# Binding one stage's weight conversion to its place in each engine's order, and three smaller edits, in a fused attention and feed-forward kernel

## The chip, the cores and the metric

One core of one Trainium2 chip. The metric is device time in microseconds (us) of one launch of the kernel, the median of several runs. TensorE (PE, with PEld for its weight loads) does the matrix products, VectorE (DVE) and ScalarE (ACT) the elementwise work, and SyncE (SP) issues every data transfer of this kernel, in order, from one queue.

## The reference, cut to what matters

```python
# attention: 4 batches, 8 heads, 512 local and 32 global tokens, head size 64
out_g = softmax(q_g @ k_all.T / 8) @ v_all                  # global queries see every key
out_l = softmax([q_l @ k_g.T, masked(q_l @ k_l.T)] / 8) @ v # local ones: |i - j| <= 32, and the global keys
x = rows(out_g, out_l)                                      # 2304 tokens x 512

h = x @ w_in                                                # layer 1: 512 -> 2048 -> 512
x = (np.maximum(h, 0.0) + alpha * np.minimum(h, 0.0)) @ w_out

h = x @ w_in2                                               # layer 2, with its own weights
return (h * np.clip(h + 3.0, 0.0, 6.0) / 6.0) @ w_out2
```

The weights arrive as 64-bit floats, the rest as 32-bit.

## The kernel before, in words

A matrix operand is held in two parts, a high one (rounded to TensorE's 32-bit form) and a low one (the remainder), and one product is three matrix products of the parts. Weights are first made 32-bit floats from the two words of each 64-bit number (`to_float32`, L100: ACT L108, then DVE L111, L112, L114), then split (ACT cast, DVE subtract).

Layer 1 goes over the tokens in five blocks (main loop, L776 to L828) of 512, 512, 512, 256 and 384 columns. A block's step s computes `h` (PE, L365) for one of 16 chunks of the hidden width; `act` (L370) takes it through ACT L375, DVE L377, ACT L383 and DVE L384 into a split tile `g`; two steps later (`LAG`) `y` (PE, L396) adds that chunk's share to four banks. Between the steps `attention_steps` issues pieces of the attention of later blocks: scores (L184), softmax (DVE L192, ACT L196), transposes (L207, copied by ACT L209 into `pt`), values (L219, scaled by DVE L223). At a block's end the attention results are transposed (L350) and split (L336, L337) into `xt` for the next block, and the four `y` banks are copied out (`evacuate`, L402: ACT L407 and DVE L405 in turn, through the ring of tiles `t`, TB = 3) and stored in DRAM, one store for each bank (L827). Block 0 also converts layer 1's own weights, which stay on the chip. Block 3 carries the global attention, and block 4 the splits (`inputs`, L552) that layer 2 starts from.

Layer 2's weights are converted during layer 1 by a generator, `second_weights` (L449): 32 chunks, each loaded (L97), converted, split and stored back to DRAM (L468) for layer 2 to read. The first 16 chunks go in pairs and make two more tiles per pair (`parts`; L471 adds, L459 cast, L462 subtract). The main loop draws some of its 158 pieces at each step; `SPLIT` = (0, 46, 46, 30, 37) says how many in each block. Layer 2 (L659) is TensorE work over these stored parts, and `rest` (L741 to L759) treats the last block's 384 tokens and ends the kernel (L634, `to_rows` L637).

Three rings of buffers matter: `raw`, four tiles that the loaded weights, the `parts` tiles and later some of layer 2's weights share; `z`, two; and `g`, three.

The order in which each engine executes is not the order of the code. The context is made with a timeline simulation (L883), and the scheduler puts each engine's instructions in the order in which that simulation finds them ready, so a piece of the generator may stand well ahead of the block step behind which it was drawn.

Of the kernel before, what the change touches and what calls it, by code (L numbers as in the profile page):

```python
# [9 lines left out]
F32 = mybir.dt.float32  # L10
F32R = mybir.dt.float32r
U32 = mybir.dt.uint32
I64 = mybir.dt.int64
AF = mybir.ActivationFunctionType
ALU = mybir.AluOpType
# [7 lines left out]
NC = DM // 128  # L23
# [4 lines left out]
UNIT_K = 15 * W  # L28

LAG = 2  # L30
# [3 lines left out]
PRE = 3  # L34
# [1 line left out]
SKEW = 1  # L36
ZB = 2
WARM = 8
TB = 3
DELAY = 4  # L40
STEPS = [[2] * 4 + [1] * 16, [1] * 16, [1] * 16, [2] * 16, [0] * 16]
CONVERT = (5, 7, 9)
# [10 lines left out]
def fused_kernel(ctx, tc, qT, kE, vE, qgT, kN, vN, vgN, w1, alpha, w2, mask, ident, out):  # L53
    nc = tc.nc
# [4 lines left out]
    work = pool("work")  # L59
# [37 lines left out]
        nc.sync.dma_start(out=raw, in_=src[j, :, 512 * m:512 * m + 512])  # L97
        return raw

    def to_float32(raw):  # L100

        words = raw.bitcast(U32).rearrange("p (f two) -> p f two", two=2)
        low, high = words[:, :, 0], words[:, :, 1]
        nc.scalar.activation(low, low, AF.Relu, bias=quarter_sb, scale=0.9 * 2.0 ** -29)  # L108
        z = work.tile([128, 512], F32, tag="z", name="z", bufs=ZB)
        bits = z.bitcast(U32)  # L110
        nc.vector.tensor_scalar(out=z, in0=high.bitcast(F32), scalar1=2.0 ** -112, scalar2=None, op0=ALU.mult)  # L111
        nc.vector.scalar_tensor_tensor(out=bits, in0=bits, scalar=3, in1=low, op0=ALU.logical_shift_left,  # L112
                                       op1=ALU.bitwise_or)
        nc.vector.scalar_tensor_tensor(out=bits, in0=high, scalar=0x80000000, in1=bits, op0=ALU.bitwise_and,  # L114
                                       op1=ALU.bitwise_or)
        return z
# [41 lines left out]
    def local_units(att):  # L158
        units = [(b, hf, hp) for b in range(B) for hf in range(2) for hp in range(HP)]
        q_t, k_t, v_t, p_t, rs_t, pt_t = {}, {}, {}, {}, {}, {}  # L160
        def load(u):
            b, hf, hp = units[u]
            q_t[u] = att.tile([128, 256], F32, tag="q", name="q_t", bufs=PRE + 1)
            nc.sync.dma_start(out=q_t[u], in_=qT[b, hp, :, 256 * hf:256 * hf + 256])
            k_t[u] = att.tile([128, UNIT_K], F32, tag="kE", name="k_t", bufs=PRE)
            nc.sync.dma_start(out=k_t[u], in_=kE[b, hp, :, 384 * hf:384 * hf + UNIT_K])

        def load_v(u):
# [61 lines left out]
        n = len(units)  # L230
# [217 lines left out]

    def second_weights():  # L449

        todo = [(j, 0) for j in range(NJ)] + [(j, 1) for j in range(NJ)]
        raws, pending = [], []

        def fetch():
            if todo:
                raws.append(load_raw(w2, *todo.pop(0)))

        def high(z, st):
            nc.scalar.copy(st[:, 0:512], z)  # L459

        def low(z, st, dst):
            nc.vector.tensor_tensor(out=st[:, 512:1024], in0=z, in1=st[:, 0:512].bitcast(F32), op=ALU.subtract)  # L462
            pending.append((dst, st))

        def store():
            if pending:
                d, st = pending.pop(0)
                nc.sync.dma_start(out=d, in_=st.bitcast(F32))  # L468

        def add(out, a, b, op=ALU.add):  # L470
            nc.vector.tensor_tensor(out=out, in0=a, in1=b, op=op)  # L471

        def parts_tile():
            return work.tile([128, 512], I64, tag="raw", name="parts", bufs=RAW).bitcast(F32R)

        fetch()
        yield
        fetch()  # L480
        for _ in range(5):
            yield
        for m in range(NP):
            own = raws.pop(0)
            z0, own = to_float32(own), own.bitcast(F32R)
            yield
            high(z0, own)
            yield
            low(z0, own, in_parts[m][:, 0])
            yield  # L490
            own = raws.pop(0)
            z1, own = to_float32(own), own.bitcast(F32R)
            store()
            yield
            high(z1, own)
            yield
            low(z1, own, in_parts[m][:, 1])
            yield
            a, b, c, d = z0[:, 0:256], z0[:, 256:512], z1[:, 0:256], z1[:, 256:512]
            add(d, c, d)  # L500
            add(c, a, c, ALU.subtract)
            store()
            yield
            st = parts_tile()
            high(z1, st)
            yield
            low(z1, st, in_parts[m][:, 2])
            fetch()
            yield
            add(a, d, a, ALU.subtract)  # L510
            add(b, b, a, ALU.subtract)
            store()
            yield
            st = parts_tile()
            high(z0, st)
            yield
            low(z0, st, in_parts[m][:, 3])
            fetch()
            yield
            store()  # L520
            yield
        for j in range(NJ):
            own = raws.pop(0)
            z, own = to_float32(own), own.bitcast(F32R)
            store()
            yield
            high(z, own)
            fetch()
            yield
            low(z, own, out_parts[j])  # L530
            yield
        store()
# [87 lines left out]
    def take(*key):  # L620
        ahead(STREAM + RAW - 2)
        return stream["got"].pop(key)
# [5 lines left out]
        nc.scalar.copy(g[:, 0, :], t)  # L628
        nc.vector.tensor_tensor(out=g[:, 1, :], in0=t, in1=g[:, 0, :].bitcast(F32), op=ALU.subtract)

    def outputs(y, g, wo, j):
        for c in range(len(y)):
            for wl, gl in ((0, 0), (1, 0), (0, 1)):
                nc.tensor.matmul(y[c], lhsT=g[:, gl, 128 * c:128 * c + 128], rhs=wo[:, wl, :],  # L634
                                 start=j == 0 and (wl, gl) == (0, 0), stop=j == NJ - 1 and (wl, gl) == (0, 1))

    def to_rows(y, tiles):  # L637
        for c, tile_ in enumerate(tiles):
            r = evacuate(y[c], c, 512, ("t", "z"))
            if tile_ == "g":  # L640
                nc.sync.dma_start(out=rows[:, 0:SG, :], in_=r)
            else:
                bb, hf, i = tile_
                at = SG + 256 * hf + 128 * i
                nc.sync.dma_start(out=rows[bb, at:at + 128, :], in_=r)
# [13 lines left out]
    def second_layer(bt):  # L659
# [14 lines left out]
        for n, two in enumerate(twos):  # L674
# [4 lines left out]
            gs, far = {}, []  # L679
# [65 lines left out]
        for j in range(NJ + LAG):  # L745
            if j < NJ:
                wt = take("in", n, j // 2, j % 2)
                h = fresh("h_ps")[:, 0:w]
                k = 0
                for c in range(NC):  # L750
                    for wl, xl in ((0, 0), (1, 0), (0, 1)):
                        nc.tensor.matmul(h, lhsT=wt[:, wl, 128 * c:128 * c + 128], rhs=xt[c][:, xl, 0:w], start=k == 0,  # L752
                                         stop=k == 3 * NC - 1)
                        k += 1
                gs[j] = g_tile()[:, :, 0:w]
                act2(h, gs[j], w)
            if j >= LAG:
                outputs(y, gs.pop(j - LAG), take("out", n, 0, j - LAG), j - LAG)
        to_rows(y, [(3, 1, 0), (3, 1, 1), "g"])  # L759

    W1 = Weights(w1, early=True)
    second, bt = second_weights(), {}
# [13 lines left out]
    for bi in range(len(blocks)):  # L776
# [43 lines left out]
        if last:  # L820
# [2 lines left out]
            for _ in more:  # L823
                pass
            ahead(STREAM + RAW - 2)
        for c in range(NC):
            nc.sync.dma_start(out=x2[bi][:, c, :], in_=evacuate(y[c], c, n)[:, :n])  # L827
        xt = xt_next  # L828

    second_layer(bt)  # L830
# [56 lines left out]
```

## Time and profile before

| | us |
|---|---|
| median of 3 runs | 899.4 (898.88 to 900.55) |
| the profiled execution | 899.25 |
| its span in the trace | 897.5 |
| PE busy in the span | 853.2 (95%) |
| DVE, ACT busy | 527.6 (59%), 392.2 (44%) |
| PE busy, 0 to 60 us (start of attention) | 49.15 |
| 60 to 165 (block 0) | 98.78 of 105 |
| 165 to 294 and 294 to 403 (blocks 1 and 2) | 114.45 of 129, 105.38 of 109 |
| 403 to 467.9 and 467.9 to 535 (blocks 3 and 4) | 64.23 of 64.9, 67.10 of 67.1 |
| 535 to 822 (layer 2), 822 to 889.2 (`rest`) | 286.86 of 287, 67.20 of 67.2 |
| mean granted TensorE clock | 0.974 |

The span is the traced part of one execution. A row of the timeline gives an instruction's start and length; the bracket at its end is the idle time of its engine just before it and what ended that. PEclk is the TensorE clock that was granted, as a share of full speed. "DMA raw<-in_w" is a load of a weight chunk, "DMA x<-ev" a store of a block's result.

### The profile page before, as it was taken

How to read it: one execution, taken by the hardware profiler on the slowest of the kernel's cores; microseconds unless marked ns; L12 is line 12 of the kernel's file. 1: busy time of each engine (PE TensorE's matmuls, PEld its weight loads, DVE VectorE, ACT ScalarE, POOL GpSimd, SP SyncE). 2: the span in 40 equal slices, each digit the busy share in tenths (PEclk: the TensorE clock that was granted, in tenths of full speed). 3: DMA queues.
4: the chain of work that ended last, by engine and by line, in shares of the span. 5: the costliest groups of instructions: out<-in, count | busy, mean ns of one | idle time of the engine just before them, and what ended most of it. 6: DMA issues, size and time to landing. Idle time of an engine off the chain costs nothing.

```text
span 897.5 us, 17192 instructions
## 1 busy us (share of the span) xinstructions
PE 853.2 (95%) x6728; PEld 736.8 (82%) x6728; DVE 527.6 (59%) x1267; ACT 392.2 (44%) x893; POOL 0.2 (0%) x4
## 2 busy tenths in 40 slices
PE   7889989898988899999999999999999999999996
PEld 5669988776766677888899998888888999988895
DVE  4988988787777874234545627665750666711221
ACT  5767565565455563324434424333430433411221
POOL 0000000000000000000000000000000000000000
PEclk7889999999999999999999999999999999999998
DMA  9885666796879984035441206565786888898881
GB/s 310 300 286 181 201 222 220 267 289 246 287 255 298 309 310 145 3 136 180 157 159 30 60 27 217 194 224 194 231 288 230 286 281 267 277 309 288 259 257 42
DMA packets 64804, 195.64 MB, mean 218 GB/s; under 512 B 7380, under 2 KB 19924, under 8 KB 63700
## 3 DMA queue, kind: packets, MB, share of 16 engines
q1 hardware_dynamic: 64724, 194.55, 65.1%
q8 instruction: 53, 0.87, 0.4%
q14 instruction: 27, 0.22, 0.1%
HBM read 160.44 MB, written 34.08 MB: 217 GB/s over the span
## 4 chain that ended last, share of the span: by engine, by line
PE 69%; DMA 16%; DVE 7%; ACT 4%; issue 2%; SPq 1%; ACTq 0%; DVEq 0%
PE o_ps L634 21%; PE k_ps L687 14%; PE h_ps L365 13%; PE y_ps L396 12%; DMA raw<-in_w 10%; PE h_ps L752 4%; DMA wi<-raw 3%; DMA wo<-raw 2%; DVE z L114 1%; DVE z L112 1%; ACT raw L108 1%; DVE t L377 1%; PE s_ps L184 1%; PE pt_ps L207 1%; PE o_ps L219 1%
## 5 line engine op out<-in xcount | busy, mean ns | idle before, releaser
L365 PE MATMUL h_ps<-xt,wt 128*128 128x256 f32 (+2 forms) x1152 | 212.4, 335 | 10.2 <-DVE xt L337 5.1
L396 PE MATMUL y_ps<-g,wt 128*128 128x256 f32 (+2 forms) x1152 | 215.8, 337 | 2.0 <-ACT g L383 2.0
L365 PEld LDWEIGHTS h_ps<-xt,wt 128*128 128x128 f32 x1152 | 181.7, 195 | 28.9 <-DVE xt L337 6.4
L396 PEld LDWEIGHTS y_ps<-g,wt 128*128 128x128 f32 x1152 | 178.2, 192 | 20.2 <-ACT g L383 2.6
L687 PE MATMUL k_ps<-bt,ws 128*128 128x512 f32 (+1 forms) x672 | 140.6, 362 | 0.0
L687 PEld LDWEIGHTS k_ps<-bt,ws 128*128 128x128 f32 x672 | 122.1, 188 | 14.3
L634 PE MATMUL o_ps<-ws,g 128*128 128x512 f32 x480 | 118.2, 391 | 0.1
L634 PEld LDWEIGHTS o_ps<-ws,g 128*128 128x128 f32 x480 | 89.6, 188 | 17.7 <-DMA ws<-wo 0.5
L377 DVE SCALAR_TENSOR_TENSOR t<-t,c_sb,h_ps 128x256 f32<-128x256 f32 (+2 forms) x96 | 55.4, 588 | 64.8 <-ACT t L375 64.4
L375 ACT ACTIVATE t<-h_ps 128x512 f32<-128x512 f32 (+2 forms) x84 | 43.2, 515 | 84.3 <-PE h_ps L365 79.4
L108 ACT ACTIVATE raw<-raw,quarter_sb 128x512 uint32<-128x512 uint32 x64 | 49.9, 781 | 66.4 <-DMA raw<-in_w 63.0
L634 PE MATMUL o_ps<-ws,far 128*128 128x512 f32 x336 | 76.8, 389 | 0.0
L634 PEld LDWEIGHTS o_ps<-ws,far 128*128 128x128 f32 x336 | 63.1, 188 | 13.1
L383 ACT CAST g<-t 128x512 fp32r<-128x512 f32 (+2 forms) x84 | 45.2, 538 | 31.7 <-DVE t L377 31.5
L384 DVE TENSOR_TENSOR g<-t,g 128x512 fp32r<-128x512 f32 (+2 forms) x84 | 49.1, 585 | 16.7 <-ACT g L383 16.2
L626 ACT ACTIVATE t<-cd,half_sb 128x512 f32<-128x512 f32 (+1 forms) x32 | 21.4, 670 | 79.8 <-DVE cd L672 79.8
L196 ACT ACTIVATE p<-p,st 128x128 f32<-128x128 f32 x128 | 49.9, 391 | 8.6 <-DVE st L192 8.6
L111 DVE TENSOR_SCALAR z<-raw 128x512 f32<-128x512 f32 x64 | 27.1, 423 | 36.0 <-DMA raw<-in_w 35.8
L112 DVE SCALAR_TENSOR_TENSOR z<-z,raw 128x512 uint32<-128x512 uint32 x64 | 44.0, 687 | 3.4 <-ACT raw L108 3.1
L114 DVE SCALAR_TENSOR_TENSOR z<-raw,z 128x512 uint32<-128x512 uint32 x64 | 43.8, 684 | 0.3
L405 DVE COPY ev<-o_ps 128x512 f32<-128x512 f32 x7 | 4.8, 689 | 66.0 <-PE o_ps L634 66.0
L184 PE MATMUL s_ps<-k_t,q_t 64*32 64x128 f32 x1024 | 30.1, 286 | 9.3 <-ACT pt L209 6.4
(97 smaller groups left out, 828.9 us busy)
## 6 DMA issues: line engine op xcount, KB each, us to landing
ws<-wi SPq DMA_DIRECT2D x80, 512.0 KB, 4.8
ws<-wo SPq DMA_DIRECT2D x80, 512.0 KB, 4.6
raw<-in_w SPq DMA_DIRECT2D x64, 512.0 KB, 5.1
v_t<-in_vE SPq DMA_DIRECT2D x32, 512.0 KB, 5.8
wi<-raw SPq DMA_DIRECT2D x16, 512.0 KB, 3.6
wi<-parts SPq DMA_DIRECT2D x16, 512.0 KB, 6.4
wo<-raw SPq DMA_DIRECT2D x16, 512.0 KB, 6.6
k_t<-in_kE SPq DMA_DIRECT2D x32, 240.0 KB, 4.8
```

Of the source, the lines that this page charges most:

```text
L108: nc.scalar.activation(low, low, AF.Relu, bias=quarter_sb, scale=0.9 * 2.0 ** -29)
L112: nc.vector.scalar_tensor_tensor(out=bits, in0=bits, scalar=3, in1=low, op0=ALU.logical_shift_left, op1=ALU.bitwise_or)
L114: nc.vector.scalar_tensor_tensor(out=bits, in0=high, scalar=0x80000000, in1=bits, op0=ALU.bitwise_and, op1=ALU.bitwise_or)
L196: nc.scalar.activation(p[:, n, :], p[:, n, :], AF.Exp, bias=st[:, 1, n:n + 1], scale=-1.0, accum_out=st[:, 2, n:n + 1])
L365: nc.tensor.matmul(ps[:, a:b], lhsT=wts[j][:, 0, wl, 128 * c:128 * c + 128], rhs=xt[c][:, xl, a:b], start=k == 0, stop=k == 3 * NC - 1)
L375: nc.scalar.activation(t[:, a:b], ps[:, a:b], AF.Relu, scale=-1.0)
L377: nc.vector.scalar_tensor_tensor(out=t[:, c:d], in0=t[:, c:d], scalar=c1_sb[:, j:j + 1], in1=ps[:, c:d], op0=ALU.mult, op1=ALU.add)
L383: nc.scalar.copy(g[:, 0, a:b], t[:, a:b])
L384: nc.vector.tensor_tensor(out=g[:, 1, a:b], in0=t[:, a:b], in1=g[:, 0, a:b].bitcast(F32), op=ALU.subtract)
L396: nc.tensor.matmul(y[c][:, a:b], lhsT=wts[j][:, 1, wl, 128 * c:128 * c + 128], rhs=g[:, gl, a:b], start=first, stop=last)
L634: nc.tensor.matmul(y[c], lhsT=g[:, gl, 128 * c:128 * c + 128], rhs=wo[:, wl, :], start=j == 0 and (wl, gl) == (0, 0), stop=j == NJ - 1 and ...
L687: nc.tensor.matmul(bank, lhsT=wt[:, wl, at:at + 128], rhs=bt[x][:, c, xl, 0:w], start=k == 0, stop=k == 5)
```

## The change

Five edits.

1. In `second_weights` the ACT, DVE and SP instructions of the conversion pass through `tc.keep_in_program_order`, which places an instruction behind the one of its engine that the code issued before it. It sets an order, not a wait. The loads (L97) and the two DVE steps L112 and L114 are not bound.
2. The ring of key tiles `k_t` has four buffers, not three.
3. TB is 2, not 3.
4. The results of a layer 1 block leave through tiles of the `g` ring: ACT copies one bank and DVE the next into one tile, and one store of 512 KB takes both (blocks of 512 columns; less for the narrower ones). A block has two stores and not four.
5. In `rest` the banks are finished, copied and stored in the order 2, 0, 1; bank 2 holds the global tokens.

```diff
-TB = 3
+TB = 2
-    def to_float32(raw):
+    def to_float32(raw, here=lambda ins: ins):
-        nc.scalar.activation(low, low, AF.Relu, bias=quarter_sb, scale=0.9 * 2.0 ** -29)
+        here(nc.scalar.activation(low, low, AF.Relu, bias=quarter_sb, scale=0.9 * 2.0 ** -29))
-        nc.vector.tensor_scalar(out=z, in0=high.bitcast(F32), scalar1=2.0 ** -112, scalar2=None, op0=ALU.mult)
+        here(nc.vector.tensor_scalar(out=z, in0=high.bitcast(F32), scalar1=2.0 ** -112, scalar2=None, op0=ALU.mult))
...
-            k_t[u] = att.tile([128, UNIT_K], F32, tag="kE", name="k_t", bufs=PRE)
+            k_t[u] = att.tile([128, UNIT_K], F32, tag="kE", name="k_t", bufs=PRE + 1)
...
     def second_weights():
+        here = tc.keep_in_program_order
...
-            nc.scalar.copy(st[:, 0:512], z)
+            here(nc.scalar.copy(st[:, 0:512], z))
-            nc.vector.tensor_tensor(out=st[:, 512:1024], in0=z, in1=st[:, 0:512].bitcast(F32), op=ALU.subtract)
+            here(nc.vector.tensor_tensor(out=st[:, 512:1024], in0=z, in1=st[:, 0:512].bitcast(F32), op=ALU.subtract))
-                nc.sync.dma_start(out=d, in_=st.bitcast(F32))
+                here(nc.sync.dma_start(out=d, in_=st.bitcast(F32)))
-            nc.vector.tensor_tensor(out=out, in0=a, in1=b, op=op)
+            here(nc.vector.tensor_tensor(out=out, in0=a, in1=b, op=op))
...
-            z0, own = to_float32(own), own.bitcast(F32R)
+            z0, own = to_float32(own, here), own.bitcast(F32R)
...
-    def outputs(y, g, wo, j):
-        for c in range(len(y)):
+    def outputs(y, g, wo, j, order=None):
+        for c in order or range(len(y)):
...
-    def to_rows(y, tiles):
-        for c, tile_ in enumerate(tiles):
+    def to_rows(y, tiles, order=None):
+        for c in order or range(len(tiles)):
+            tile_ = tiles[c]
...
-                outputs(y, gs.pop(j - LAG), take("out", n, 0, j - LAG), j - LAG)
-        to_rows(y, [(3, 1, 0), (3, 1, 1), "g"])
+                outputs(y, gs.pop(j - LAG), take("out", n, 0, j - LAG), j - LAG, (2, 0, 1))
+        to_rows(y, [(3, 1, 0), (3, 1, 1), "g"], (2, 0, 1))
...
-        for c in range(NC):
-            nc.sync.dma_start(out=x2[bi][:, c, :], in_=evacuate(y[c], c, n)[:, :n])
+        for c in range(0, NC, 2):
+            r = work.tile([128, 2, 512], F32, tag="g", name="ev", bufs=LAG + 1)[:, :, :n]
+            nc.scalar.copy(r[:, 0, :], y[c][:, :n])
+            nc.vector.tensor_copy(r[:, 1, :], y[c + 1][:, :n])
+            nc.sync.dma_start(out=x2[bi][:, c:c + 2, :], in_=r)
```

What this does to the engines' order shows at three places. The first is VectorE at the border of blocks 0 and 1, before: `z` and `parts` belong to the conversion of layer 2's weights, `xt` is the split input of block 1, `ev` a result of block 0 on its way out.

```order
L462 TENSOR_TENSOR parts<-z,parts 128x512
L223 TENSOR_TENSOR xo<-o_ps,rs 128x256
L384 TENSOR_TENSOR g<-t,g 128x256
L111 TENSOR_SCALAR z<-raw 128x512 x2
L112 SCALAR_TENSOR_TENSOR z<-z,raw 128x512
L198 TENSOR_SCALAR st<-st 128x4
L337 TENSOR_TENSOR xt<-xt_ps,xt 128x512
L114 SCALAR_TENSOR_TENSOR z<-raw,z 128x512
L200 RECIPROCAL rs<-st 128x4
L112 SCALAR_TENSOR_TENSOR z<-z,raw 128x512
L337 TENSOR_TENSOR xt<-xt_ps,xt 128x512 x3
L114 SCALAR_TENSOR_TENSOR z<-raw,z 128x512
```

The same border, VectorE, in the changed kernel (L832 is the new copy of the results):

```order
L384 TENSOR_TENSOR g<-t,g 128x256
L223 TENSOR_TENSOR xo<-o_ps,rs 128x256
L198 TENSOR_SCALAR st<-st 128x4
L200 RECIPROCAL rs<-st 128x4
L337 TENSOR_TENSOR xt<-xt_ps,xt 128x512 x4
L832 COPY ev<-y_ps 128x512 x2
L377 SCALAR_TENSOR_TENSOR t<-t,c_sb,h_ps 128x512
L384 TENSOR_TENSOR g<-t,g 128x512
```

The conversion has moved from in front of the four `xt` splits to later in block 1. The second place is VectorE in the middle of block 4. Before, only `act` (L377, L384) and the splits for layer 2 (L561, L564) stand there:

```order
L561 TENSOR_TENSOR bt<-xq,bt 128x512
L377 SCALAR_TENSOR_TENSOR t<-t,c_sb,h_ps 128x384
L384 TENSOR_TENSOR g<-t,g 128x384
L561 TENSOR_TENSOR bt<-xt,bt 128x512
L564 TENSOR_TENSOR xt<-xq,xt 128x512
L561 TENSOR_TENSOR bt<-xq,bt 128x512
L377 SCALAR_TENSOR_TENSOR t<-t,c_sb,h_ps 128x384
L384 TENSOR_TENSOR g<-t,g 128x384
```

In the changed kernel, block 4 (L563 and L566 are the lines L561 and L564 of before; L111, L112, L114 and L463 are the conversion):

```order
L566 TENSOR_TENSOR xt<-xt,xq 128x512
L563 TENSOR_TENSOR bt<-xq,bt 128x512
L384 TENSOR_TENSOR g<-t,g 128x384
L114 SCALAR_TENSOR_TENSOR z<-raw,z 128x512
L377 SCALAR_TENSOR_TENSOR t<-t,c_sb,h_ps 128x384
L463 TENSOR_TENSOR raw<-z,raw 128x512
L563 TENSOR_TENSOR bt<-xt,bt 128x512
L384 TENSOR_TENSOR g<-t,g 128x384
L111 TENSOR_SCALAR z<-raw 128x512
L377 SCALAR_TENSOR_TENSOR t<-t,c_sb,h_ps 128x384
L112 SCALAR_TENSOR_TENSOR z<-z,raw 128x512
L384 TENSOR_TENSOR g<-t,g 128x384
```

About one chunk of the conversion now stands between any two splits of `g` there; in all, the last 12 of the 32 chunks are converted in block 4. The third place is SyncE in block 1 of the changed kernel, where each store of the conversion (L469, `wi_...`) is bound and the loads of the attention units stand behind it:

```order
L469 DMA wi_100<-raw 128x1024
L97 DMA raw<-in_w 128x512
L164 DMA q_t<-in_qT 128x256
L166 DMA k_t<-in_kE 128x480
L171 DMA v_t<-in_vE 128x1024
L469 DMA wi_100<-parts 128x1024
L97 DMA raw<-in_w 128x512
L469 DMA wi_100<-parts 128x1024
```

Before, in the same block, two units with six transfers of the conversion between them and more on either side:

```order
L171 DMA v_t<-in_vE 128x1024
L468 DMA wi_102<-raw 128x1024
L97 DMA raw<-in_w 128x512 x2
L468 DMA wi_102<-parts 128x1024 x2
L468 DMA wi_103<-raw 128x1024
L166 DMA k_t<-in_kE 128x480
L164 DMA q_t<-in_qT 128x256
```

Between two units there are now about three transfers of the conversion; the loads of seven units stand behind such a store.

## Rows read from the trace of the kernel before

**Rows 1.** Stages: stretch, length, busy PE, PEld, DVE, ACT, POOL, PEclk, DMA share, GB/s
```profile
165.00:294.00 129.00, 114.45 (x967) 90.73 (x966) 96.90 (x243) 73.22 (x167) 0.00 (x0) 0.95 0.82 277
...
403.00:467.90 64.90, 64.23 (x878) 57.88 (x878) 31.19 (x104) 26.35 (x77) 0.00 (x0) 1.00 0.51 170
467.90:535.00 67.10, 67.10 (x387) 66.80 (x386) 32.85 (x57) 25.28 (x50) 0.00 (x0) 1.00 0.13 36
```

**Rows 2.** TensorE's waits, 165 to 330 us: total, times, longest
```profile
PE s_ps L184 <- ACT pt L209: 6.4, 3, 3.1
PE o_ps L219 <- DVE t L377: 3.9, 2, 2.0
PE xt_ps L350 <- DVE t L377: 3.8, 1, 3.8
PE h_ps L365 <- DVE xt L337: 3.5, 2, 3.1
```

**Rows 3.** ScalarE's timeline in block 1
```profile
217.41 0.77 ACT L108 ACTIVATE raw<-raw,quarter_sb 128x512 uint32<-128x512 uint32 x1 [5.76 <-DMA raw<-in_w]
```

**Rows 4.** TensorE's timeline in block 1
```profile
219.19 0.64 PE L184 MATMUL s_ps<-k_t,q_t 64*32 64x128 f32 x22 [3.07 <-ACT pt L209]
...
220.55 6.43 PE L396 MATMUL y_ps<-g,wt 128*128 128x512 f32 x21
...
234.72 5.06 PE L396 MATMUL y_ps<-g,wt 128*128 128x512 f32 x21
```

**Rows 5.** Windows of 20 us, columns as in rows 1
```profile
80.00:100.00 20.00, 19.45 (x268) 18.44 (x267) 17.90 (x48) 13.07 (x29) 0.00 (x0) 1.00 0.63 193
100.00:120.00 20.00, 17.99 (x203) 17.39 (x203) 17.85 (x47) 12.68 (x32) 0.00 (x0) 1.00 0.68 227
120.00:140.00 20.00, 19.31 (x267) 18.29 (x266) 18.46 (x44) 12.64 (x27) 0.00 (x0) 1.00 0.47 156
...
160.00:180.00 20.00, 16.04 (x188) 13.13 (x170) 15.65 (x40) 11.51 (x28) 0.00 (x0) 0.91 0.81 282
...
300.00:320.00 20.00, 16.38 (x182) 12.50 (x181) 16.78 (x44) 13.47 (x31) 0.00 (x0) 0.91 0.96 320
```

**Rows 6.** VectorE's and TensorE's timelines at the border of blocks 2 and 3
```profile
403.65 0.69 DVE L405 COPY ev<-y_ps 128x512 f32<-128x512 f32 x1 [2.27 <-DMA x<-ev]
...
401.86 1.59 PE L365 MATMUL h_ps<-xt,wt 128*128 128x256 f32 x12
...
405.40 1.69 PE L365 MATMUL h_ps<-xt,wt 128*128 128x256 f32 x12 [0.67 <-DVE t L377]
...
408.84 1.69 PE L396 MATMUL y_ps<-g,wt 128*128 128x256 f32 x12
```

**Rows 7.** DMA issues: count, KB each, median us from issue to landing
```profile
raw<-in_w SPq DMA_DIRECT2D x64, 512.0 KB, 5.1
...
wo<-raw SPq DMA_DIRECT2D x16, 512.0 KB, 6.6
...
x<-ev SPq DMA_DIRECT2D x12, 256.0 KB, 3.1
```

**Rows 8.** TensorE's timeline in the first 60 us
```profile
7.11 0.64 PE L184 MATMUL s_ps<-k_t,q_t 64*32 64x128 f32 x16 [1.66 <-DMA k_t<-in_kE]
...
24.71 0.65 PE L219 MATMUL o_ps<-v_t,pt 128*32 128x64 f32 x32 [1.41 <-DMA v_t<-in_vE]
```

**Rows 9.** VectorE by line and form: count, busy, mean ns, idle before
```profile
L112 DVE SCALAR_TENSOR_TENSOR z<-z,raw 128x512 uint32<-128x512 uint32 x64 | 44.0, 687 | 3.4 <-ACT raw L108 3.1
...
L111 DVE TENSOR_SCALAR z<-raw 128x512 f32<-128x512 f32 x64 | 27.1, 423 | 36.0 <-DMA raw<-in_w 35.8
L462 DVE TENSOR_TENSOR raw<-z,raw 128x512 fp32r<-128x512 f32 x32 | 21.9, 687 | 1.7 <-ACT raw L459 1.5
```

**Rows 10.** SyncE's timeline at the end
```profile
890.36 0.70 SPq L641 DMA_DIRECT2D out<-ev  x1
```

More of the change, by code (lines that the diff above doesn't have):

```diff
@@ L491, in second_weights @@
             own = raws.pop(0)
-            z1, own = to_float32(own), own.bitcast(F32R)
+            z1, own = to_float32(own, here), own.bitcast(F32R)
             store()
@@ L523, in second_weights @@
             own = raws.pop(0)
-            z, own = to_float32(own), own.bitcast(F32R)
+            z, own = to_float32(own, here), own.bitcast(F32R)
             store()
```

## The prediction

> **What bounds the kernel now.** I read the busy shares by stage first. Layer 2 and `rest` are full of TensorE work (the table above), and so are blocks 3 and 4: 64.23 of 64.9 us and 67.10 of 67.1 [rows 1]. There is no idle time to win there. Between 165 and 294 us TensorE is busy 114.45 of 129, and its granted clock is below full. The gap lies here.
>
> TensorE's waits in 165 to 330 us name what it waits for: `pt` of ACT 6.4 us, `t` of DVE 3.9 and 3.8, `xt` of DVE 3.5, together 17.6 [rows 2]. None of these is slow in itself, so I went to the timeline of the engine named. Before the longest wait for `pt`, ACT stands 5.76 us at L108, the first step of a weight conversion, until a chunk `raw` has landed [rows 3]. The copy into `pt` is two instructions behind it, and TensorE's scores stop for 3.07 us [rows 4]. DVE has the same at L111: 35.8 us of idle time in the whole kernel before that line, ended by a load [rows 9], and at the border of blocks 0 and 1 two L111 stand ahead of the `xt` splits (the first order above). Thus work that layer 2 needs 200 us later keeps work waiting that TensorE needs at once. DVE is far from full there, 96.90 of 129 [rows 1]: this is an order that is wrong, not a load that is too large.
>
> These stops have a second price. The 21 products of `y` just behind the 3.07 us stop take 6.43 us, and 21 like them 5.06 in an undisturbed step, 1.37 less [rows 4]. Five of the eight windows of 20 us from 160 to 320 show a granted clock of 0.91 (the first and the last in [rows 5]): the lower level, 1.2 instead of 2.4 GHz, for part of the window, each time behind an idle stretch of two us or more.
>
> **The change part by part**, in us of the profiled span of 897.5. That execution's time is 899.25, so 1.75 lie outside; the median, 899.4, is 0.15 above it.
>
> *Conversion bound to its place, blocks 1 and 2.* Nothing is added or removed; the instructions come later. The four `xt` splits come directly behind the attention's rows (second order). The conversion of a chunk comes at least three pieces behind the issue of its load, and with 46 pieces in a block of 109 to 129 us a piece is 2.4 to 2.8 us, so 7 us or more against 5.1 from issue to landing [rows 7]. So most of the 17.6 goes. What is late next is PE itself; I keep 2 for a load that lands late in a busy stretch: **-15.6**. Bounds: -17.6 if no stop is left, -8.8 if half of them return at other instructions.
>
> *Clock.* Five falls by 1.37 are 6.9; one remains with the 2 us kept: **-5.5**. Bounds -6.9 and -2.7 (three remain).
>
> *Results through `g`, TB 2.* At the border of blocks 2 and 3 DVE's copy L405 waited 2.27 us for a store to give back its `t` tile, and `act` behind it cost PE 0.67 [rows 6]. This wait goes: **-0.7** (0 to -0.7). In its place `act` of a block's second step needs a `g` tile that the pair store must first release. At that border the first `h` starts at 401.86, when the last bank is done, and `y` of the second step starts at 408.84 [rows 6]. Copy 0.69, store, then half of `act`, some 0.8: the store may take 408.84 - 401.86 - 1.5 = 5.5. A 256 KB store lands in 3.1 and a 512 KB one of the conversion in 6.6 [rows 7]; by the second PE is 1.1 late. At the wider borders a step is longer and covers even that. I take **+0.3** (0 to +1.1), since fewer transfers are in flight at this border than where the 6.6 was measured.
> By the Trainium skill, "DMA: Bandwidth & Descriptors", section "Anatomy of one DMA", a transfer is 2.0 us fixed plus its bytes at 436 KB per us, so an estimate of 3.2 us for 512 KB; that term would be 0, though the section gives this fit for the GpSimd path and says that a write to HBM may take surprisingly long, as 6.6 against the 5.1 of a load bears out.
>
> *Fourth key tile.* It lets a key load be issued one unit earlier. In the first 60 us TensorE waited 1.66 for `k_t` and 1.41 for `v_t` [rows 8], but an earlier key load goes ahead of other loads of the same queue. **0** (+3.1 to -3.1, the two waits once more, or gone).
>
> *What the conversion costs where it goes.* In block 4 the last 12 chunks stand among the splits (fourth order). A chunk is L111 0.42, L112, L114 (like L112) and the split at 0.69 each [rows 9]: 2.49, times 12 is 29.9. With 32.85 DVE is then busy 62.7 of 67.1, 94%; ACT has room (25.28 of 67.1) [rows 1]. The trace has no block 4 like that. Its nearest rows are 80 to 140 us, where DVE is busy 17.85 to 18.46 of 20: there PE idles 0.55, 2.01 and 0.69, on average 1.08 [rows 5], which over 67.1 us is **+3.6**. Bounds: 0, since `g` is wanted two steps after its `h` and that slack absorbs a queue; and 2.01 per 20, 6.7, with one fall of the clock, 8.1. In block 3, 30 pieces are ten chunks at most, 25 us; 31.19 + 25 is 56 of 64.9, 87%, less than in any of those three windows: **+0.5** (0 to 1.08 per 20, 3.5).
>
> *Order of the last banks.* Before, the last transfer to be issued, of the global tile, starts at 890.36 and takes 0.70 to issue [rows 10]; now it goes first and the issue of a shorter list ends the kernel; of the 0.70 I take about half. **-0.4** (0 to -0.7).
>
> Sum: -15.6 - 5.5 - 0.7 + 0.3 + 0 + 3.6 + 0.5 - 0.4 = **-17.8**. Span 879.7, with 1.75 an execution of 881.4, and with the median's 0.15, 881.6. I say 881.5.
>
> **Rivals.**
> A. VectorE becomes the bound in blocks 3 and 4. For it: 94%, and a bound order means that `act` cannot pass a conversion that waits for its load. Against: `g` has two steps of slack, about 8 us, and in rows 5 the loss at such a load is small. With both upper bounds, 8.1 + 3.5 in place of 4.1, the gain is 10.3: 889.
> B. The stops only partly go: a bound L108 still waits at its new place whenever its load is late, and `pt` or `t` stand behind it. With half of the 17.6 (-8.8) and two falls fewer (-2.7) instead of -21.1, the sum is -8.2: 891.
> C, the other side: SyncE's queue. A bound store cannot be passed, and it waits for the DVE subtract of its chunk. Seven units' loads stand behind such stores. If a store is held up longer than the units' loads lead, `k_t` and `v_t` are late. As priced in the first 60 us that is 1.66 + 1.41 = 3.07 for a unit [rows 8], 21.5 for seven: 881.5 + 21.5 = 903. It decides from 17.8 / 3.07, about six of the seven. For it: only `raw` loads and these stores share the queue, and DVE does run late at times. Against: the fourth key tile lets loads lead by one more unit, and the stores were in the same queue before without a wait of TensorE for a load in rows 2.
> D. The change does not do what it says. The orders exclude that for the moves; what remains of it is in B.
>
> **How the numbers follow.** The forecast's own case 0.62, its range 870 (all lower bounds: -17.6 - 6.9 - 0.7 - 3.1 - 0.7 = -29.0) to 887. A 0.16, B 0.12, C 0.05, and 0.05 for A and B together (889 and the 9.6 by which B's 11.5 fall short of 21.1, some 899). The range takes in A and B, from 870 to 893, and leaves out C, A with B, and tails of the others, together under 0.2. A measurement of this kernel can tell 0.2%, 1.8 us, from no change. Faster by more: 0.62 + 0.15 + 0.11 = 0.88. Within it: 0.02 of A and B, 0.03 of both together, 0.05. Slower: C and 0.02 of both together, 0.07.
>
> **What would show it right or wrong.** Right: in 165 to 330 us TensorE's waits sum to about 2 instead of 17.6, ACT's L108 and DVE's L111 no longer idle for loads by several us, and the clock windows of 0.91 fall from five to about one; blocks 1 and 2 together are some 20 us shorter. In block 4 DVE is busy about 63 us and the block is 2 to 5 us longer than 67.1. The first 60 us and layer 2 stay within 3 us. Wrong: waits of TensorE for `pt` and `t` behind L108 and L111 at new places (B), `y` waiting for `g` of DVE through blocks 3 and 4, or layer 2 starting late (A), or `s_ps` and `o_ps` waiting for `k_t` and `v_t` (C). A total above 893 says that one of these decides.

## The result, and the profile after

The changed kernel takes 877.0 us (median of 4 runs, 875.57 to 878.08) and the kernel before 900.0 beside it: ratio 0.9745, interval 0.9723 to 0.9766. The forecast was 881.5, in a range of 870 to 893. The profiled execution takes 876.12 and its span is 874.3: 23.2 shorter than before, where I had worked out 17.8.

The stages of the changed kernel, cut where each block's first `h` starts (stretch, length, busy PE, PEld, DVE, ACT, POOL, granted clock, DMA share, GB/s): blocks 1, 2, 3 and 4, layer 2, and the tail.

```profile
162.80:266.70 103.90, 103.90 (x946) 83.40 (x945) 58.97 (x166) 49.28 (x128) 0.00 (x0) 1.00 0.47 157
266.70:368.10 101.40, 101.40 (x870) 81.35 (x868) 59.29 (x157) 46.81 (x114) 0.00 (x0) 1.00 0.52 177
368.10:436.10 68.00, 65.59 (x881) 58.36 (x880) 47.32 (x136) 35.42 (x93) 0.00 (x0) 1.00 0.82 285
436.10:511.00 74.90, 71.11 (x398) 69.97 (x398) 59.29 (x109) 37.89 (x73) 0.00 (x0) 0.98 0.66 213
511.00:799.30 288.30, 286.63 (x1338) 246.08 (x1337) 158.88 (x278) 97.32 (x173) 0.00 (x0) 1.00 0.78 258
866.30:874.30 8.00, 0.03 (x1) 0.00 (x0) 0.69 (x1) 0.75 (x2) 0.00 (x0) 0.71 0.36 98
```

Blocks 1 and 2 of the kernel before, cut in the same way:

```profile
170.90:294.60 123.70, 112.22 (x944) 88.61 (x945) 95.36 (x239) 70.45 (x161) 0.00 (x0) 0.94 0.81 275
294.60:401.90 107.30, 103.68 (x870) 82.72 (x869) 55.95 (x146) 46.01 (x112) 0.00 (x0) 0.98 0.51 175
```

In the changed kernel TensorE is busy in blocks 1 and 2 without a gap (103.90 of 103.90, 101.40 of 101.40), at the full clock. The waits of [rows 2], 17.6 us, are all gone, and neither L108 nor L111 waits for a load there. The same products are also faster: 1814 matmul records before hold 112.22 + 103.68 = 215.9 us of busy time, 1816 now 205.3. VectorE's work there fell from 151.3 to 118.3 us, since part of the conversion went to blocks 3 and 4, and those are now longer. By the starts of L111, one for each chunk, blocks 0 to 4 convert 6, 18, 8, 0 and 0 of layer 2's 32 chunks before and 0, 6, 7, 6 and 12 after; the last one starts at 512.43 us, in layer 2. The account of the 23.2, span against span:

| stretch | before | after | difference | forecast |
|---|---|---|---|---|
| start to the end of block 0's `y` | 167.8 | 162.8 | -5.0 | 0 |
| from there to the end of block 2 | 234.1 | 205.3 | -28.8 | -21.8 |
| block 3 | 64.2 | 68.0 | +3.8 | +0.8 |
| block 4 | 69.8 | 74.9 | +5.1 | +3.6 |
| layer 2 | 286.3 | 288.3 | +2.0 | 0 |
| `rest` | 67.0 | 67.0 | 0 | 0 |
| tail | 8.3 | 8.0 | -0.3 | -0.4 |

The forecast came within 5 us partly by luck, because two errors of opposite sign fell together: 12 us more were gained, and 6.5 more were given back. So the experiments ask two things: which edit gains, and what the price in blocks 3 and 4 is.

Three stops of TensorE belong to block 4 and the start of layer 2 of the changed kernel:

```profile
482.52 3.06 PE L396 MATMUL y_ps<-g,wt 128*128 128x384 f32 x12 [1.91 <-ACT g L383]
...
508.68 2.37 PE L396 MATMUL y_ps<-g,wt 128*128 128x384 f32 x12 [1.88 <-ACT g L383]
...
527.98 3.02 PE L636 MATMUL o_ps<-ws,g 128*128 128x512 f32 x12 [1.64 <-DMA ws<-wo]
```

ScalarE's timeline ahead of the first two: each time an instruction that waits for a transfer, with the `g` casts behind it (the second is a bound one, L108).

```profile
477.64 0.62 ACT L562 CAST bt<-xq 128x512 fp32r<-128x512 f32 x1 [4.68 <-DMA xq<-x]
...
505.57 0.76 ACT L108 ACTIVATE raw<-raw,quarter_sb 128x512 uint32<-128x512 uint32 x1 [5.03 <-DMA raw<-in_w]
```

SyncE's timeline, the same places:

```profile
466.47 0.33 SPq L469 DMA_DIRECT2D wo<-raw  x1
471.92 0.33 SPq L97 DMA_DIRECT2D raw<-in_w  x1
472.33 1.02 SPq L547 DMA_DIRECT2D xq<-x  x2
...
496.18 0.32 SPq L469 DMA_DIRECT2D wo<-raw  x1
500.86 0.33 SPq L97 DMA_DIRECT2D raw<-in_w  x1
```

From 466.8 to 471.92 the queue issues nothing. A load L97 follows the store of 466.47 some 5 us later, as the load of 500.86 follows the store of 496.18: it needs one of the four `raw` tiles, and the median store of this kind takes 5.0 us to land. The `xq` loads that ACT waits for stand behind it. SyncE's waits in 436 to 511 us (total, times, longest) name the same:

```profile
SPq L97 <- DMA wo<-raw: 38.0, 12, 5.7
```

So a late conversion does not only cost VectorE time; it stands in the one queue through which layer 2's inputs and weights come.

### The profile page after: what moved, and what is told of

Read it like the earlier page. It is cut to its first block, busy times and chain, and to the rows that moved or that the text cites. A ratio compares the mean times of both kernels' runs of the same rounds, so it can differ in the third digit from the quotient of the medians.

```text
span 874.3 us, 17112 instructions
## 1 busy us (share of the span) xinstructions
PE 843.5 (96%) x6728; PEld 731.1 (84%) x6728; DVE 527.2 (60%) x1267; ACT 388.9 (44%) x893; POOL 0.2 (0%) x4
## 4 chain that ended last, share of the span: by engine, by line
PE 75%; DMA 11%; DVE 8%; ACT 4%; issue 1%; SPq 1%; ACTq 0%; DVEq 0%
PE o_ps L636 21%; PE h_ps L365 15%; PE y_ps L396 14%; PE k_ps L690 14%; DMA raw<-in_w 5%; PE h_ps L755 4%; DMA wo<-raw 3%; PE s_ps L184 2%; DVE z L112 1%; PE o_ps L219 1%; PE pt_ps L207 1%; DVE z L114 1%; DVE t L377 1%; ACT raw L108 1%; DMA ws<-wi 1%
## 5 line engine op out<-in xcount | busy, mean ns | idle before, releaser
L396 PE MATMUL y_ps<-g,wt 128*128 128x256 f32 (+2 forms) x1152 | 212.4, 334 | 7.2 <-ACT g L383 7.2
L365 PE MATMUL h_ps<-xt,wt 128*128 128x256 f32 (+2 forms) x1152 | 209.9, 333 | 3.7 <-DVE t L377 3.0
L396 PEld LDWEIGHTS y_ps<-g,wt 128*128 128x128 f32 x1152 | 175.3, 190 | 26.8 <-ACT g L383 8.9
L636 PE MATMUL o_ps<-ws,g 128*128 128x512 f32 x480 | 117.8, 391 | 1.6 <-DMA ws<-wo 1.6
L377 DVE SCALAR_TENSOR_TENSOR t<-t,c_sb,h_ps 128x256 f32<-128x256 f32 (+2 forms) x96 | 55.4, 589 | 76.9 <-ACT t L375 76.9
L108 ACT ACTIVATE raw<-raw,quarter_sb 128x512 uint32<-128x512 uint32 x64 | 49.0, 768 | 28.4 <-DMA raw<-in_w 28.4
L384 DVE TENSOR_TENSOR g<-t,g 128x512 fp32r<-128x512 f32 (+2 forms) x84 | 49.2, 586 | 19.2 <-ACT g L383 19.1
L112 DVE SCALAR_TENSOR_TENSOR z<-z,raw 128x512 uint32<-128x512 uint32 x64 | 44.0, 688 | 2.2 <-ACT raw L108 0.9
L114 DVE SCALAR_TENSOR_TENSOR z<-raw,z 128x512 uint32<-128x512 uint32 x64 | 43.9, 686 | 0.6
L630 ACT CAST g<-t 128x384 fp32r<-128x384 f32 (+1 forms) x48 | 26.3, 549 | 26.4 <-DVE t L629 26.4
L631 DVE TENSOR_TENSOR g<-t,g 128x384 fp32r<-128x384 f32 (+1 forms) x48 | 28.8, 600 | 12.4 <-ACT g L630 11.3
```

Of the source, the lines that this page charges most:

```text
L108: here(nc.scalar.activation(low, low, AF.Relu, bias=quarter_sb, scale=0.9 * 2.0 ** -29))
L365: nc.tensor.matmul(ps[:, a:b], lhsT=wts[j][:, 0, wl, 128 * c:128 * c + 128], rhs=xt[c][:, xl, a:b], start=k == 0, stop=k == 3 * NC - 1)
L377: nc.vector.scalar_tensor_tensor(out=t[:, c:d], in0=t[:, c:d], scalar=c1_sb[:, j:j + 1], in1=ps[:, c:d], op0=ALU.mult, op1=ALU.add)
L384: nc.vector.tensor_tensor(out=g[:, 1, a:b], in0=t[:, a:b], in1=g[:, 0, a:b].bitcast(F32), op=ALU.subtract)
L396: nc.tensor.matmul(y[c][:, a:b], lhsT=wts[j][:, 1, wl, 128 * c:128 * c + 128], rhs=g[:, gl, a:b], start=first, stop=last)
```

## The experiments

Each was timed beside the kernel before. A stage length comes from one profiled execution.

**The bound order alone.** The kernel before with edit 1 only.

```diff
 # before, and in second_weights:
+        here = tc.keep_in_program_order   # around L108, L111, casts, subtracts, adds, stores
```

> The kernel before with the bound order of the conversion alone (three key tiles, TB 3, four stores for each block, old order of the last banks). Theory: the bound order is what ends the stops of blocks 1 and 2 and delays the conversion out of block 0, so it carries nearly all of the 22.9 us: 876 to 881, blocks 1 and 2 together some 205 us as in the changed kernel. Rival: the stores through g and the fourth key tile carry a good part of it: 885 to 896.

Measured: 875.5 us, ratio 0.9742 (0.9706 to 0.9777), the same as the whole change. Blocks 1 and 2 take 104.1 and 101.5 us. The bound order carries the gain; the other four edits add nothing to it that these runs can tell. Which of the three engines' bindings it needs was not run. Block 4 and layer 2 of this kernel:

```profile
438.00:508.40 70.40, 69.15 (x398) 68.52 (x397) 61.94 (x114) 40.63 (x77) 0.00 (x0) 1.00 0.68 232
508.40:794.30 285.90, 285.90 (x1337) 246.18 (x1337) 156.22 (x273) 94.48 (x169) 0.00 (x0) 1.00 0.76 259
```

VectorE is busy 61.94 of 70.40 us, 88%, more than the 79% of the changed kernel, and the block pays nearly nothing (69.8 before). VectorE's load by itself is not the price. This profile is of the fastest of the six runs (871.19 us); whether block 4 pays as little in the others is not shown.

**The four other edits alone.**

```diff
 # after
-        here = tc.keep_in_program_order
+        here = lambda ins: ins
```

> The changed kernel without the bound order (four key tiles, results through g, TB 2, new order of the last banks stay). Theory: all the stops behind L108 and L111 come back, 896 to 900, with TensorE waiting some 15 us or more in 165 to 330 us. Rival: the other four edits carry a part, 885 to 893.

Measured: 891.2 us, ratio 0.9915 (0.9889 to 0.9941), between the two and in the rival's range. The stops are back, fewer of them; the longest in TensorE's timeline:

```profile
170.40 3.78 PE L365 MATMUL h_ps<-xt,wt 128*128 128x512 f32 x8 [4.29 <-DVE xt L337]
...
279.07 1.11 PE L350 MATMUL xt_ps<-ident_sb,xo 128*128 128x128 f32 x4 [3.94 <-DVE t L377]
...
296.60 0.64 PE L184 MATMUL s_ps<-k_t,q_t 64*32 64x128 f32 x16 [1.71 <-ACT pt L209]
```

The first is the border of blocks 0 and 1 again. Without the bound order the four edits gain 8.4 us in stops of the floating conversion (block 1 117.8 us against 123.7); with it there is nothing left of that to gain.

**The stores through `g` alone**, on the kernel before.

```diff
 # before
-        for c in range(NC):
-            nc.sync.dma_start(out=x2[bi][:, c, :], in_=evacuate(y[c], c, n)[:, :n])
+        for c in range(0, NC, 2):   # as in the change: one g tile, two copies, one store
```

> The kernel before with the results through g (one store for two banks) and nothing else of the change; TB 3, three key tiles, conversion not bound. The four smaller edits without the bound order took 891.2 against 899.6. Theory: fewer transfers in SyncE's queue and another order of the free-floating conversion give that, and the stores are the part that shifts it: 891 to 895. Rival: the fourth key tile gives it: 898 to 901 here.

Measured: 894.5 us, ratio 0.9949 (0.9931 to 0.9968): about half of the 8.4, and in the theory's range. The rest was not divided further.

**No conversion in block 4.**

```diff
 # after
-SPLIT = (0, 46, 46, 30, 37)
+SPLIT = (0, 62, 62, 34, 0)
```

> The changed kernel with the pieces of the conversion drawn as (0, 62, 62, 34, 0) and not (0, 46, 46, 30, 37): none left for block 4. Theory: block 4 and the start of layer 2 pay 7.1 us for the conversion that stands there, VectorE at 59.6 of 75.9 us; TensorE is full in blocks 1 and 2 with VectorE below 60%, so more work there costs nothing: 869 to 873, with block 4 back at 69 to 70 us. Rival: the bound order itself costs it (a bound instruction waits in the way wherever it stands), and with more pieces in a step the stops come back in blocks 1 and 2: 876 to 884.

Measured: 876.2 us, ratio 0.9759 (0.9728 to 0.9789), no gain. Blocks 3 and 4 and layer 2:

```profile
373.60:451.10 77.50, 70.78 (x882) 60.70 (x881) 55.56 (x150) 40.05 (x100) 0.00 (x0) 0.96 0.84 297
451.10:519.90 68.80, 68.80 (x398) 68.50 (x397) 39.36 (x69) 29.06 (x57) 0.00 (x0) 1.00 0.32 103
519.90:805.70 285.80, 285.80 (x1338) 246.31 (x1337) 155.79 (x271) 94.61 (x169) 0.00 (x0) 1.00 0.74 251
```

Half of the theory holds: block 4 and layer 2 together take 354.6 in place of 363.2, and blocks 1 and 2 stay full, which the rival did not expect. But block 3 takes 77.5 in place of 68.0 and gives it all back. The profile is of the slowest of the six runs (882.56 us; the other five take 875.3 to 880.1): its first block ends 5.4 us later than the changed kernel's, and how long block 3 is in a run of 876 was not seen.

**Still earlier.**

```diff
 # after
-SPLIT = (0, 46, 46, 30, 37)
+SPLIT = (0, 70, 70, 18, 0)
```

> The changed kernel with the pieces drawn as (0, 70, 70, 18, 0). With 62 in each of blocks 1 and 2 these stayed full, and block 3 took 77.5 us with loads that landed late in front of bound steps. Theory: block 3's price comes from the conversion that stands there; with 18 pieces in place of 34 it falls to some 68 us, and blocks 1 and 2 stay near 104 and 101.4: 866 to 871. Rival: the bound steps stop TensorE wherever a load is late, and at 70 pieces a load has less lead in blocks 1 and 2 too, so the stops return there: 874 to 882.

Measured: 877.3 us, ratio 0.9767 (0.9744 to 0.9789). Blocks 1 and 2 stay full:

```profile
165.00:368.40 203.40, 203.40 (x1803) 162.77 (x1802) 144.16 (x369) 108.10 (x262) 0.00 (x0) 1.00 0.65 221
```

They convert 22 chunks here, one every 9.2 us, against 26 in the kernel before, one every 8.9, and 13 in the changed one. So the smaller number of chunks is not what ends the stops of these blocks. The time lies in the rival's range, but its mechanism is not seen there.

Block 3 again takes 77.5, of which 2.9 are twelve `y` products of block 2 that stand behind the first `h`. The run does not test the pieces as it was meant to: the conversion lags behind the drawing, and with 18 pieces in place of 34 L111 still starts 10 times in block 3 in place of 12. Windows of 10 us of this kernel, at the start of block 3:

```profile
366.00:376.00 10.00, 10.00 (x76) 7.08 (x75) 6.74 (x13) 4.80 (x9) 0.00 (x0) 1.00 0.99 384
376.00:386.00 10.00, 7.63 (x109) 6.81 (x111) 8.72 (x27) 6.86 (x19) 0.00 (x0) 1.00 0.99 306
```

The DMA engines are busy 0.99 of the time: the global attention's keys and values (1 MB each) and the conversion's loads and stores come together. In the changed kernel the same two windows have 0.65 and 0.91. But in the first of the two TensorE is full, and of its 6.3 us of idle time in block 3 only 1.7 are a wait for such a load (`gk`, at 407.03).

**All in blocks 1 and 2.**

```diff
 # after
-SPLIT = (0, 46, 46, 30, 37)
+SPLIT = (0, 79, 79, 0, 0)
```

> The changed kernel with all pieces in blocks 1 and 2, (0, 79, 79, 0, 0). Theory: blocks 3, 4 and layer 2 return to their times of before (64.2, 69.8, 286), since VectorE's and the queue's work there is gone; blocks 1 and 2 stay near 104 and 101 as VectorE would be busy some 81% there: 864 to 868. Rival: a piece now lasts 1.3 us, so five pieces from load to use are 6.5 us against 4.7 to landing, and the bound steps wait for late loads: TensorE idles 5 to 15 us in blocks 1 and 2, 872 to 880.

Measured: 894.0 us, ratio 0.9950 (0.9928 to 0.9972): nearly the whole gain is gone. The bound order is the same; by the drawing a chunk of the last 16 (three pieces each) comes every 3.9 us now, while the loads go out some 5.9 us apart. The waits between 160 and 400 us (total, times, longest) are of the kind of the kernel before:

```profile
ACT raw L108 <- DMA raw<-in_w: 33.4, 16, 8.6
...
DVE z L111 <- DMA raw<-in_w: 16.7, 9, 7.8
...
PE xt_ps L350 <- DVE t L377: 8.4, 2, 5.6
```

They do not lie where they lay before. TensorE is full from 166.8 to 326.8 us, also in the last 40 us, where six chunks start, one every 6.7 us and so as densely as in block 1 before (18 in 123.7 us). It stops mostly at the border of blocks 2 and 3, where the global attention's loads come too, and in block 3:

```profile
286.80:326.80 40.00, 40.00 (x403) 31.60 (x406) 33.34 (x84) 25.15 (x59) 0.00 (x0) 1.00 0.73 247
366.80:383.00 16.20, 8.45 (x31) 6.61 (x31) 9.30 (x19) 6.83 (x13) 0.00 (x0) 0.78 0.57 187
...
400.94 2.93 PE L365 MATMUL h_ps<-xt,wt 128*128 128x256 f32 x12 [9.19 <-DVE t L377]
```

Ahead of the last, L108 and L111 wait 8.6 and 7.8 us for one load, which itself waited 8.4 us in the queue for a store. Block 3 takes 82.7 us although no piece is drawn there: four chunks are still converted in it. It is the rival's mechanism, bound steps that wait for late loads, but neither range held the time. The order helps only as long as the loads land before their places.

**More in block 4.**

```diff
 # after
-SPLIT = (0, 46, 46, 30, 37)
+SPLIT = (0, 36, 36, 30, 57)
```

> The changed kernel with the pieces drawn as (0, 36, 36, 30, 57): 20 more pieces, some seven chunks and 17 us of VectorE, in block 4. Theory: block 4 has about 8 us of VectorE left to give, so it grows by some 9 us and more with the waits between the engines: 884 to 892. Rival: the price of block 4 is not VectorE's load but single late transfers, which do not grow with the load: 876 to 880.

Measured: 900.9 us, ratio 1.0012 (0.9990 to 1.0035). Block 4 takes 79.8 us, layer 2 307.1. Block 4 converts 13 chunks, one more than in the changed kernel; four more start in layer 2's time. Waits in 438 to 560 us:

```profile
ACT raw L108 <- DMA raw<-in_w: 33.7, 13, 4.6
PE k_ps L690 <- DMA ws<-wi: 16.9, 2, 15.9
```

The larger part of the price is not in the block: layer 2's first weights are loaded behind the last conversions, and TensorE waits 15.9 us at once. The size outgrew my theory (884 to 892), which had counted VectorE only.

**Three `t` tiles again** (and three key tiles).

```diff
 # after
-TB = 2
+TB = 3
-bufs=PRE + 1   # k_t
+bufs=PRE
```

> The changed kernel with TB 3 and three key tiles: bound order, results through g and the new order of the last banks stay. In the run with the bound order alone, block 4 took 70.4 us and layer 2 286.0, here 74.9 and 288.3. Theory: with two t tiles and block 4's VectorE this full, act of one step waits for that of the one before it, so TB 3 gives back some 4 to 6 us: 870 to 874. Rival: the difference is the order that the stores through g make, or scatter from one execution to another: 875 to 878.

Measured: 877.6 us, ratio 0.9768 (0.9742 to 0.9794): no gain, the rival holds. Block 4 takes 71.5 and layer 2 289.0, still longer than with the old stores.

**A fifth `raw` tile.** The room comes from `v_t` (two in place of three) and the mask.

```diff
 # after
-RAW = 4
+RAW = 5
-bufs=3   # v_t
+bufs=2
```

> The changed kernel with five raw tiles instead of four (RAW = 5; two v tiles instead of three and the mask in the attention's pool make room). In block 4 of the changed kernel the last load was issued at 500.86 us, 4.7 us after the store at 496.18 that freed its tile; ACT's L108 waited 5.03 us for it and g's cast and TensorE's y stood behind. Theory now: the price of blocks 3 and 4 is these loads that wait for a tile in front of bound steps, not VectorE's load; a fifth tile lets each load start one chunk earlier: block 4 and layer 2 return from 363.2 towards 356, 868 to 872 in all. Rival, the forecast's own term: VectorE, 59 of 75 us busy there, is the price, which a fifth tile does not change: 875 to 879.

Measured: 879.4 us, ratio 0.9784 (0.9755 to 0.9814). The waits of L108 for loads in 366 to 535 us fall to 1.8 us, but block 4 still takes 74.2 and layer 2 288.6:

```profile
440.60:514.80 74.20, 72.03 (x407) 71.34 (x406) 61.51 (x113) 40.50 (x80) 0.00 (x0) 0.98 0.65 215
```

As a theory of the whole price, the missing tile falls. SyncE still waits 34.2 us in block 4 for stores ahead of L97, and ACT 6.5 us for `xq`.

**The room without the tile.** Two `v_t` tiles, the mask moved, four `raw` tiles.

```diff
 # after
-bufs=3   # v_t
+bufs=2
```

> The changed kernel with two v tiles instead of three and the mask in the attention's pool, four raw tiles: the room of the run with five raw tiles without the fifth tile. Theory: v loads have slack in blocks 1 and 2 and this alone changes nothing, 875 to 879. Rival: attention waits for v, some 3 us and more: above 880.

Measured: 876.2 us, ratio 0.9749 (0.9719 to 0.9779): nothing, as expected.

**Five tiles, none in block 4.**

```diff
 # after with RAW = 5
-SPLIT = (0, 46, 46, 30, 37)
+SPLIT = (0, 66, 66, 26, 0)
```

> Five raw tiles, and the pieces drawn as (0, 66, 66, 26, 0). With four tiles 62 to 70 pieces in each of blocks 1 and 2 left these full but made block 3 77.5 us, with waits of L108 and L111 for loads. Theory: with the fifth tile a load is early enough for a chunk every 4.7 us, and block 3 falls to 66 to 70 us while block 4 and layer 2 stay as in the kernel before: 863 to 868. Rival: block 3 is limited by the transfers of the global attention (share of the DMA engines 0.83 there), which a tile does not change: 874 to 878.

Measured: 881.5 us, ratio 0.9801 (0.9773 to 0.9829): block 3 77.6 (2.9 of it block 2's last `y`), block 4 68.8, layer 2 286.0. A tile does not shorten block 3, as the rival said; that the global attention's transfers are the reason is not shown, and the time is above its range as well. Eleven chunks start in block 3 here.

**Five tiles, a middle way.**

```diff
 # after with RAW = 5
-SPLIT = (0, 46, 46, 30, 37)
+SPLIT = (0, 56, 56, 26, 20)
```

> Five raw tiles, and the pieces drawn as (0, 56, 56, 26, 20), between the changed kernel's and the early one. Theory: no block has a chunk more often than every 5.4 us, so no load is late and the price of blocks 3 and 4 falls to some 2 us: 865 to 869. Rival (transfers of block 3, or VectorE): 872 to 877.

Measured: 872.3 us, ratio 0.9701 (0.9673 to 0.9729), the fastest here, though in the rival's range and not the theory's. Blocks 3 and 4 and layer 2:

```profile
371.10:440.00 68.90, 66.42 (x874) 58.55 (x873) 49.05 (x138) 36.70 (x94) 0.00 (x0) 0.98 0.88 309
440.00:509.80 69.80, 69.80 (x406) 69.44 (x405) 51.22 (x93) 35.46 (x68) 0.00 (x0) 1.00 0.55 179
509.80:795.80 286.00, 286.00 (x1337) 246.38 (x1337) 155.48 (x271) 94.57 (x169) 0.00 (x0) 1.00 0.75 254
```

Twenty pieces in block 4, eight chunks, cost nothing there or in layer 2. Block 4 and layer 2 together, by the pieces in block 4: 354.6 with none (four tiles), 355.8 with 20 (five tiles), 363.2 with 37 (the changed kernel), 362.8 with 37 and five tiles, 386.9 with 57. All these have the stores through `g`, and among them the price goes with the count and not with the tile; whether 20 pieces with four tiles do as well was not run. But the bound order alone, with 37 pieces and the old stores, takes 356.3.

## Why the prediction came out as it did

*The stops of blocks 1 and 2* (-15.6, with 2 kept). Right in mechanism and nearly in size: all 17.6 went. The bound order alone does it, and without it most are back.

*The clock* (-5.5, bounds -6.9 and -2.7). Right in direction, too small in size: with as many matmul records TensorE's busy time in blocks 1 and 2 fell by 10.6. I priced a fall by the 21 products just behind a stop [rows 4], 1.37. A window of 20 us at 0.91 [rows 5] lacks 1.8, five of them 9.0; and the stage clocks of 0.94 and 0.98 over 123.7 and 107.3 us lack 7.4 + 2.1 = 9.6. The rows of the windows held nearly the whole price, the row of the products a part of it; the last us of the 10.6 is not accounted for. One reading was loose: the last window at 0.91, 300 to 320 us, holds no idle stretch of two us or more, only two of 1.75 and 1.87.

*The first 163 us* (0). Here a term was left out: the conversion also left block 0 (six chunks; VectorE from 93.4 busy in 60 to 170.9 us to 80.4 in 60 to 162.8). How much it is worth stays partly open, since this stretch varies from kernel to kernel: block 1 starts at 162.8 to 168.2 us in the seven profiles with the bound order, four `raw` and three `v` tiles (median 165.0), and at 170.4 to 171.2 in the three without it, a border stop of 2.9 to 4.3 included. Against the median that leaves some 1 to 3 us for block 0 itself, an estimate, and the rest of the -5.0 is scatter.

*Results through `g`* (-0.7 and +0.3). In the changed kernel a 512 KB store lands in 2.7 us:

```profile
x<-ev SPq DMA_DIRECT2D x6, 512.0 KB, 2.7
```

I took my upper bound from the conversion's 6.6 [rows 7]; no `act` waited for such a tile at the border of blocks 2 and 3. The 6.6 was the dearest row of its kind. Other stores of the same size, in the same trace of before, have:

```profile
wi<-raw SPq DMA_DIRECT2D x16, 512.0 KB, 3.6
```

So the 6.6 does not come from a write to DRAM as such, as I had read it.

By the Trainium skill, "DMA: Bandwidth & Descriptors", section "Anatomy of one DMA", the estimate was 3.2; the trace's 2.7 lies nearer to it than to the 6.6. The changed kernel's stores of the conversion, of the same size, have medians of 3.0, 4.1 and 5.0 us, so that estimate does not hold for all stores of this queue.

*Fourth key tile, order of the last banks* (0 and -0.4). Neither is shown to gain (with three key tiles and TB 3 the time is 877.6). With the bound order alone, old bank order, the tail takes 8.0 us as well.

*The price of the later place* (+3.6 in block 4, +0.5 in block 3, nothing in layer 2). This is the step that failed, in its mechanism more than in its sum of 4.1 against 10.9. I counted VectorE and took its loss at a like load from [rows 5]. The count of chunks was right in block 4 (12) and too high in block 3 (six, not ten), which costs 3.8 and not 0.5. But VectorE at 88% costs next to nothing in block 4 with the bound order alone. Shown is that with the stores through `g` the price of block 4 and layer 2 grows with the pieces (from 356 to 363 to 387 us) and that the late pieces are transfers: an `xq` load behind a load that waits for a tile, a `raw` load 5 us late, `ws` loads behind the last conversions.

The late transfer alone is not the price either. With 20 pieces and five tiles ACT waits 8.4 us for `xq` in block 4, as long as the 8.5 of the changed kernel, and TensorE loses nothing; VectorE is busy 51.2 us there. With the bound order alone VectorE is busy 61.9 us, ACT waits 1.3 for `xq`, and TensorE loses little. In the four kernels with 37 pieces and the stores through `g` both come together, VectorE at 59.2 to 61.5 and ACT's wait at 6.4 to 8.5, and all four pay. That it takes both is read from six single profiles, and no run was made to test it. It is rival A's sum (8.1 + 3.5) by rival C's mechanism, a queue that cannot be passed, with other loads than those I had named. At the border of blocks 2 and 3 VectorE was in fact full for a moment:

```profile
366.00:376.00 10.00, 8.85 (x85) 7.23 (x84) 9.53 (x22) 5.69 (x14) 0.00 (x0) 1.00 0.65 221
```

9.53 of 10 us, as the result copies, `act`, the reductions of the global attention and two chunks of the conversion meet; TensorE's 1.15 us stop at 375.18 for `g` follows from it. That is a burst, which the block's mean of 70% does not show.

*Open.* Why block 3 is long in the four kernels that leave nothing for block 4: 77.5 us with 34, 18 and 26 pieces (some 74.6 in the last two without block 2's last `y`) and 82.7 with none. The full DMA engines are seen, that they are the cause was only argued. Something else goes with it that I had not counted: L111 starts 12, 10 and 11 times in block 3 of the first three, and five to eight times in the kernels whose block 3 takes 66.9 to 69.6. The fourth, with four starts, has the stop of 9.2 us behind one late load. Also open is why block 4 with layer 2 takes 356.3 with the old stores and 360.5 to 363.2 with the stores through `g`, at 37 pieces each: these are single profiles, in kernels whose medians differ by no more than their scatter. What goes with it is SyncE's wait for stores ahead of L97 in block 4, 21.9 us with the old stores and 33.2 to 38.0 with the others.

## What to carry to other kernels

When engines wait in order for work that is not yet due, bind that work to its place before enlarging buffers; then keep the places far enough apart that each load lands before its place, which here meant about one full turn of its buffer (load, convert, store). Keeping the work away from the stretch where other loads are thick is what the stops at the border of blocks 2 and 3 suggest; no run isolates it. Count the work where the trace shows it, not where the code draws it. Price a move at the place it goes to by every resource it uses there, the transfer queue included, and not by the engine alone. Read the price of a slow clock from the granted clock of the stage, not from the first instructions behind a stop.

## What the runs showed of the hardware

In windows of 10 us with a DMA share of about 1 the DMA engines moved 384 GB/s in the kernel with 70, 70, 18 and 0 pieces (366 to 376 us), 411 in the one with five tiles and 20 pieces in block 4 (380 to 390 us), and 372 in the kernel before (10 to 20 us). So the high rate is not new with the change.

The time of the first 165 us differs by up to 5.4 us between kernels that have the same code up to there but for the later parts' order. With the bound order alone six runs spread from 871.2 to 882.7 us, so differences of a few us in single profiles have to be read by stage.
